# Attention followed by two feed-forward layers on one core: early input and weight sums around the second layer's tiles, and results leaving in other pieces

## The chip, the cores and the metric

One core of a Trainium2 chip runs the whole program. The metric is the device time of one execution in microseconds (us), the median over several runs. The engines are the matmul engine (PE, TensorE; its weight loads are listed as PEld), DVE (VectorE), ACT (ScalarE) and POOL (GpSimd); SP issues nearly all transfers, in the order of its own queue. Each engine takes its instructions in a fixed order, and an instruction that waits holds everything behind it on that engine.

## The reference

```python
attn = g * mem_out + (1 - g) * local       # 4 batches, 8 heads, 576 positions, 64 wide
x = attn.transpose(0, 2, 1, 3).reshape(2304, 512)
h = x @ w_in;   x = where(h > 0, h, exp(min(h, 0)) - 1) @ w_out     # layer 1, 512 -> 2048 -> 512
h = x @ w_in2;  out = maximum(0.01 * h, h) @ w_out2                 # layer 2, 512 -> 2048 -> 512
```

The local attention is causal, with a softmax; `mem_out` reads a memory matrix per head. Inputs and output are float32 (the weights come in as 64-bit floats and are unpacked on the chip). Only layer 2, and what is prepared for it in layer 1, is touched by the change.

## The kernel before

Every float32 operand of a matmul is split into a high part (rounded to fp32r) and a low part (the rest), and a product is made in three passes: high by high, low by high, high by low. ACT (or DVE) makes the high part as a copy, POOL (or DVE) the low part as a subtraction.

**Tiles.** After the attention, both layers run over five wide tiles of tokens, called T0 to T4 here (`gi` 0 to 4 in the code): four of 512 tokens and a last one of 256. Layer 1 goes over all five first and stores its results, x1, in DRAM (`x1_scr`, `x1s` in the trace). Then layer 2 goes over all five. The 2048 hidden columns are 16 blocks of 128, `f` = 0 to 15.

**Layer 2, plain tiles (T0, T1, T4).** For each f: 12 matmuls of 512 columns (L624) make the hidden block in a PSUM bank (tags `tp` and `pm`, two banks each); `leaky` makes its activation on ACT (L646) and DVE (L647), then the high part `gh` on DVE (L246) and the low part `gl` on POOL (L631). Two blocks later `emit_o3` feeds them into the output: four row blocks of 128 tokens, 12 matmuls of 512 columns per f (L987), into four banks (`sc` three times, `po` once) that add up over all 16 f.

**Layer 2, fast tiles (T2, T3).** Two hidden blocks are made together, as a 2 by 2 block product in seven products in place of eight (L1004; six matmuls of 256 columns each). That needs four sums of the two blocks' weights (`ws`) and four sums of the tile's inputs (the differences that `combine` makes), each again split in high and low. The products are added up on DVE (L1008) with copies on ACT; `rows` then makes the activation (L1012 DVE, L1015 ACT, L1016 POOL). In the first pair the products come in this order: a11 b11, a12 b21 (plain weights and inputs), then the ones with a weight sum: s4 b22, s1 t1, s2 t2, s3 t3, and at last a22 t4.

**What is prepared where.** `combine` (L936) runs in layer 1, one tile after T2 and T3: four DVE subtractions on the x1 tiles (L939), and four stores of the sums to DRAM (L940), per tile. `combine_w` (L948) makes the weight sums of the eight pairs of blocks during layer 2's T1, each tied behind the activation of a block f in `STEPS` = 0, 1, 2, 4, 5, 7, 8, 10. Each uses the one `wm` buffer: two additions (L955) and four of half the size (L957) on DVE, a copy on ACT (L960) into one of two input buffers (`xw1`, `xv1`), two subtractions on POOL (L962), a store to DRAM (L965). `load_ws` (L970) brings the sums of a pair back into one of the two `wraw` buffers; the first two pairs are loaded right at f = 0 and 1 of T1, the others two pairs ahead of their use.

**From one tile to the next.** `load3` (L851) is emitted near the end of a tile. It loads x1 of the next tile into the buffers `y` and `x` (L861; one buffer each) and splits it into `xh`, `xl` (L848 ACT, L849 POOL and DVE), which lie in `xw1`, `xv1` for all tiles but T1, and there in `xw0`, `xv0`. For a fast tile it then loads the input sums into the same `y` and `x` (L871) and splits them into `xw0`, `xv0`, all low parts on POOL. At a tile's end eight copies (L1081, DVE, 128 by 256 each) take the output banks through two `st` buffers to DRAM (L1082).

**Who sets the order.** The program is emitted in the order of the code; the framework then orders each engine's instructions by a simulated timeline and by priority, so that a load can be issued earlier than its place in the code. `behind_elu` (L879) keeps what it emits behind the last activation's instructions on the same engine.

Of the kernel before, what the change touches and what calls it, by code (L numbers as in the profile page):

```python
# [8 lines left out]
F32 = mybir.dt.float32  # L9
F32R = mybir.dt.float32r  # L10
# [9 lines left out]
def _f(ap):  # L20
    return ap.bitcast(F32)
# [3 lines left out]
def kernel(  # L25
# [135 lines left out]
    FAST = (2, 3)  # L161
    xt_scr = {gi: dram.tile([P, 4, 2, TW // 2], F32, name=f"xt{gi}") for gi in FAST}
    ws_scr = [dram.tile([P, 2, 4, 2 * P], F32, name=f"ws{i}") for i in range(NPR)]
# [687 lines left out]
    def load3(gi):  # L851
        w = wide[gi][1]
        xh, xl = (mtile(tag, 1, F32R, (NKC, TW))[:, :, 0:w] for tag in (("xw0", "xv0") if gi == 1 else ("xw1", "xv1")))
        for o in range(0, w if gi == 0 else 0, TN):
            st = mtile("x", 1, F32, (NKC, TN))
            nc.sync.dma_start(st, x1_scr[gi][:, :, o:o + TN])
            for c in range(NKC):
                split_to(xh[:, c, o:o + TN], xl[:, c, o:o + TN], st[:, c], nc.gpsimd)
        for e in range(2 if gi else 0):
            st = mtile("yx"[e], 1, F32, (2, w))  # L860
            nc.sync.dma_start(st, x1_scr[gi][:, 2 * e:2 * e + 2])  # L861
            for c in range(2):
                split_to(xh[:, 2 * e + c], xl[:, 2 * e + c], st[:, c], nc.vector if e else nc.gpsimd)
        if gi not in FAST:
            return xh, xl, None
        sums = []
        for e, tag in enumerate(("xw0", "xv0")):
            t = mtile(tag, 1, F32R, (NKC, TW)).rearrange("p a n -> p (a n)")
            t = t.rearrange("p (k l c n) -> p k l c n", k=2, l=2, c=2)
            st = mtile("yx"[e], 1, F32, (2, 2, TW // 2))  # L870
            nc.sync.dma_start(st, xt_scr[gi][:, 2 * e:2 * e + 2])  # L871
            for k in range(2):
                split_to(t[:, k, 0], t[:, k, 1], st[:, k], nc.gpsimd)
                sums.append((t[:, k, 0], t[:, k, 1]))
        return xh, xl, sums

    later = []

# [8 lines left out]
    for gi, (t0, w) in enumerate(wide):  # L887
# [9 lines left out]

        ys, yts = [], []

        def fetch_y():  # L900
            ne = NKC * TN // w
            for e in range(NKC // ne):
# [7 lines left out]
                ys.extend(yt[:, i] for i in range(ne))  # L910
                yts.append(yt)

        for f in range(NFA, NF):
# [6 lines left out]
            gs[f] = elu(ph, w)  # L920
            if later and f == NFA + (gi < 4):
                behind_elu(later.pop())
            if f > NFA + 1:
# [11 lines left out]

        def combine(gi=gi, yts=yts):  # L936
            b = [y[:, :, o:o + TW // 2] for y in yts for o in (0, TW // 2)]
            for k, o, x, y in ((0, 0, 1, 0), (3, 1, 3, 1), (1, 3, 3, 0), (2, 2, 2, 3)):
                nc.vector.tensor_tensor(out=b[o], in0=b[x], in1=b[y], op=ALU.subtract)  # L939
                nc.sync.dma_start(xt_scr[gi][:, k], b[o])  # L940

        if gi in FAST:
            later.append(combine)

    for u in w2:
        u()

    def combine_w(pr):  # L948

        m = pools["wst"].tile([P, 2 * DM], I32, tag="wm", bufs=pools["nwm"], name="wm")  # L950
        t = _f(m).rearrange("p (k n) -> p k n", k=4)
        for j in range(2):
# [3 lines left out]
        for o, a, b, op in ((3, 2, 3, ALU.add), (2, 0, 2, ALU.subtract), (0, 3, 0, ALU.subtract), (1, 1, 0, ALU.subtract)):  # L956
            nc.vector.tensor_tensor(out=t[:, o], in0=t[:, a], in1=t[:, b], op=op)  # L957
        v = mtile(("xw1", "xv1")[pr % 2], 1, F32R, (NKC, TW)).rearrange("p a n -> p (a n)")
        v = v.rearrange("p (l k n) -> p l k n", l=2, k=4)
        nc.scalar.copy(v[:, 0], t)  # L960
# [6 lines left out]
    uses = [(gi, pr) for gi in FAST for pr in range(NPR)]  # L967
    ws = {}

    def load_ws(key):  # L970
        raw = pools["wst"].tile([P, 2, DM, 2], I32, tag="wraw", bufs=2, name="wraw")
        v = raw.rearrange("p a n t -> p (a n t)").bitcast(F32R).rearrange("p (l k n) -> p l k n", l=2, k=4)
        nc.sync.dma_start(_f(v), ws_scr[key[1]])
        ws[key] = [v[:, :, k].rearrange("p l (c n) -> p l c n", c=2) for k in range(4)]

    STEPS = (0, 1, 2, 4, 5, 7, 8, 10)
    cur = load3(0)
    for gi, (t0, w) in enumerate(wide):
# [17 lines left out]

        xh, xl, sums = cur
        h = TW // 2
# [20 lines left out]
        for pr in range(NPR):  # L1019
            if gi in FAST:  # L1020
# [20 lines left out]
                add(u, product(a22, t4), u)  # L1041
                rows(2 * pr + 1, c1)
                at_use = uses.index((gi, pr)) + 2
                if at_use < len(uses):
                    load_ws(uses[at_use])
            else:
                for f in (2 * pr, 2 * pr + 1):
                    ph = h_bank()[:, 0:w]
                    h_mm(ph, wi_tiles[1, f], xh, xl)
                    gs[f] = leaky(ph, w)  # L1050
                    if gi == 1 and f in STEPS:
                        n = STEPS.index(f)
                        behind_elu(lambda: combine_w(n))
                        if n < 2:
                            load_ws(uses[n])
                    if f > 2 * pr and pr == NPR - 1:
                        break
                    if f > 1:
                        emit_o3(f - 2)
            if pr == NPR - 1 and gi + 1 < len(wide):  # L1060
                cur = load3(gi + 1)
            if pr == NPR - 1 or (pr and gi in FAST):
# [11 lines left out]
        for f in (NF - 2, NF - 1):  # L1074
            emit_o3(f)
        for tb in range(w // P):
            r0 = t0 + tb * P
            for hf in range(2):
                cs = slice(hf * DM // 2, (hf + 1) * DM // 2)
                o = mtile("st", 2, F32, (DM // 2,))  # L1080
                nc.vector.tensor_copy(o, pos[tb][:, cs])  # L1081
                nc.sync.dma_start(out[r0:r0 + P, cs], o)  # L1082

# [29 lines left out]
```

## Time and profile before

| | us |
|---|---|
| runs shown | 1077.43, 1077.97 (median), 1079.25 |
| the profiled execution's own time | 1078.21 |
| its span, first to last instruction | 1076.40 |
| busy time of the matmul engine in it | 1039.3 |

The profile shows one execution. "Busy" is the time in which an engine had an instruction under way; a wait is the idle time in front of an instruction, put down to what ended last before it. The granted clock of the matmul engine stands at 1.00 for 2.4 GHz and at 0.50 for 1.2 GHz; a stretch with a value between has parts at both. Layer 2 takes T1 from about 757 us on, T2 from about 845 us, T3 from about 940 us.

### The profile page before, as it was taken

The page shows a single profiled execution, that of the slowest core. Times are in us where ns is not written, and L with a number is a line of the kernel's source. Part 1 is how long each engine was busy: PE and PEld are TensorE (multiplying, and loading weights), DVE is VectorE, ACT ScalarE, POOL GpSimd, SP SyncE. Part 2 cuts the span into 40 slices and gives each one's busy share as a digit, 9 for nine tenths or more (in the row PEclk, how much of TensorE's full clock was granted, in tenths as well). Part 3 has the DMA queues.
Part 4 walks back from the last instruction along what each step waited for, and adds up shares of the span by engine and source line. Part 5 has one row for each costly group of instructions (what it writes and reads, how often), then busy time and mean ns, then how long its engine had stood idle before and what let it go on. Part 6 is the DMA issues. An engine that isn't in the chain of part 4 may idle for free. (4 is left out here: it accounts for less than half of the span.)

```text
span 1076.4 us, 18223 instructions
## 1 busy us (share of the span) xinstructions
PE 1039.3 (97%) x6192; PEld 921.6 (86%) x6192; DVE 679.3 (63%) x1524; ACT 513.7 (48%) x1223; POOL 552.7 (51%) x678
## 2 busy tenths in 40 slices
PE   6998999999999999999999999999999799999998
PEld 4776799989999999878888889788888688999897
DVE  6889987788888736566762426753565345454532
ACT  5999887787878635444442215332122221322211
POOL 7675775676767535455552217654345522432321
PEclk9999999999999999999999999999999999999999
DMA  7755543564455259456582305530252443452110
GB/s 183 196 144 117 161 140 101 128 167 141 122 128 146 90 136 342 146 194 201 186 274 79 118 4 174 176 117 0 79 195 118 133 141 107 139 159 87 40 40 20
DMA packets 154173, 144.47 MB, mean 134 GB/s; under 512 B 80608, under 2 KB 141024, under 8 KB 151008
## 3 DMA queue, kind: packets, MB, share of 16 engines
q1 hardware_dynamic: 153936, 143.04, 43.5%
q8 instruction: 49, 0.80, 0.3%
q14 instruction: 44, 0.36, 0.1%
q10 hardware_dynamic: 144, 0.26, 0.1%
HBM read 97.39 MB, written 42.34 MB: 130 GB/s over the span
## 5 line engine op out<-in xcount | busy, mean ns | idle before, releaser
L631 POOL TENSOR_TENSOR gl<-e,gh 128x512 fp32r<-128x512 f32 (+2 forms) x149 | 158.7, 1069 | 230.7 <-DVE gh L246 113.6
L987 PE MATMUL sc<-w,gh 128*128 128x512 f32 x448 | 136.7, 394 | 0.0
L454 POOL TENSOR_SCALAR pt<-pt,rs,omg 128x128 f32<-128x128 f32 (+4 forms) x160 | 103.3, 655 | 20.7 <-DVE rs L449 16.7
L624 PE MATMUL tp<-xw,w 128*128 128x512 f32 (+1 forms) x376 | 104.8, 360 | 1.5 <-DVE e L639 1.5
L624 PE MATMUL pm<-xw,w 128*128 128x512 f32 (+1 forms) x368 | 103.2, 362 | 1.2 <-ACT w L245 1.2
L439 ACT ACTIVATE pt<-pt,mx 128x128 f32<-128x128 f32 (+4 forms) x160 | 93.3, 584 | 23.0 <-DVE mx L434 21.5
L655 PE MATMUL sc<-gh,w 128*128 128x512 f32 (+2 forms) x438 | 103.2, 340 | 0.3 <-DVE gh L246 0.3
L1016 POOL TENSOR_TENSOR gl<-e,gh 128x512 fp32r<-128x512 f32 x32 | 41.6, 1300 | 114.9 <-ACT gh L1015 95.5
L987 PEld LDWEIGHTS sc<-w,gh 128*128 128x128 f32 x448 | 80.9, 190 | 13.7
L138 POOL TENSOR_TENSOR w<-wm,w 128x512 fp32r<-128x512 f32 x50 | 66.3, 1346 | 47.7 <-ACT w L245 39.5
L987 PE MATMUL sc<-w,gl 128*128 128x512 f32 x224 | 83.7, 393 | 5.1 <-POOL gl L631 5.1
L460 PE MATMUL tp<-ident,pt 128*128 128x128 f32 x480 | 83.1, 279 | 3.5 <-DVE al L253 1.5
L655 PEld LDWEIGHTS sc<-gh,w 128*128 128x128 f32 x438 | 74.6, 188 | 9.3 <-DVE gh L246 0.8
L624 PE MATMUL pm<-xh,w 128*128 128x288 f32 x368 | 80.3, 304 | 1.6 <-ACT xh L613 1.6
L624 PEld LDWEIGHTS tp<-xw,w 128*128 128x128 f32 x376 | 67.7, 189 | 13.0 <-DVE e L639 1.9
L624 PEld LDWEIGHTS pm<-xw,w 128*128 128x128 f32 x368 | 66.3, 189 | 12.7 <-ACT w L245 1.6
L434 DVE CUSTOM_DVE_ANT_0 pt<-sc,mask 128x128 f32<-128x128 f32 (+4 forms) x160 | 69.4, 445 | 7.5 <-PE sc L432 3.5
L460 PEld LDWEIGHTS tp<-ident,pt 128*128 128x128 f32 x480 | 59.6, 143 | 9.8 <-ACT ah L250 2.6
L624 PE MATMUL tp<-xv,w 128*128 128x512 f32 (+1 forms) x188 | 67.7, 360 | 0.0
L624 PE MATMUL pm<-xv,w 128*128 128x512 f32 (+1 forms) x184 | 66.5, 361 | 0.0
L655 PE MATMUL sc<-gl,w 128*128 128x512 f32 (+2 forms) x219 | 66.3, 340 | 0.2 <-POOL gl L631 0.2
L655 PE MATMUL pm<-gh,w 128*128 128x288 f32 x280 | 63.3, 306 | 0.0
(206 smaller groups left out, 2701.0 us busy)
## 6 DMA issues: line engine op xcount, KB each, us to landing
wraw<-in_moe_w_in_dram SPq DMA_DIRECT2D x32, 512.0 KB, 4.2
wraw<-in_moe_w_out_dram SPq DMA_DIRECT2D x32, 512.0 KB, 5.0
wraw<-ws SPq DMA_DIRECT2D x16, 1024.0 KB, 5.0
xh<-xh SPq DMA_DIRECT2D x8, 576.0 KB, 3.4
xl<-xl SPq DMA_DIRECT2D x8, 576.0 KB, 4.0
ys<-st SPq DMA_DIRECT2D x32, 144.0 KB, 2.8
vn<-in_v_dram SPq DMA_DIRECT2D x64, 64.0 KB, 2.6
out_dram<-st SPq DMA_DIRECT2D x32, 128.0 KB, 1.7
```

Of the source, the lines that this page charges most:

```text
L138: nc.gpsimd.tensor_tensor(out=w[:, 1, a], in0=t[:, a], in1=_f(w)[:, 0, a], op=ALU.subtract)
L434: nc.vector.tensor_tensor_reduce(out=pt[0:m, k0:k0 + n], in0=sc[0:m, 0:n], in1=mk, op0=ALU.add, op1=ALU.min, scale=-0.125, scalar=mx[0:m, ...
L439: nc.scalar.activation(out=pt[0:m, 0:nk], in_=pt[0:m, 0:nk], func=AF.Exp, scale=-1.0, bias=mx[0:m, last:last + 1], accum_out=self.pd["ss"] ...
L454: nc.gpsimd.tensor_scalar(out=pt, in0=pt, scalar1=rs[0:m, i:i + 1], scalar2=omg[0:m, h:h + 1], op0=ALU.mult, op1=ALU.mult,)
L460: nc.tensor.transpose(dst, self.p[c][:, k0:k0 + kn], ident)
L624: nc.tensor.matmul(ph, wi[:, wj, kc, :], xx[:, kc, :], start=n_mm == 0, stop=n_mm == 11)
L631: lo = nc.gpsimd.tensor_tensor(out=gl, in0=g, in1=_f(gh), op=ALU.subtract)
L655: nc.tensor.matmul(py, wo[:, wj, ec * P:(ec + 1) * P], gg, start=opens and f == first and n_mm == 0, stop=closes and f == last and n_mm == 2,)
L987: nc.tensor.matmul(pos[tb], gg[:, tb * P:(tb + 1) * P], wo[:, wj, :], start=f == 0 and n_mm == 0, stop=f == NF - 1 and n_mm == 2,)
L1016: nc.gpsimd.tensor_tensor(out=gl, in0=flat, in1=_f(gh), op=ALU.subtract)
```

## The change

In layer 1 `combine` goes. Everything else is in layer 2:

- During T1, behind f = 1, `sums_ahead` loads x1 of T3 into `y` and `x`, makes its four sums there in place and stores them to DRAM. Behind f = 3, `inputs_ahead` loads x1 of T2 into the same buffers, splits it into `xw1`, `xv1`, and makes T2's sums in place in `y` and `x`, where they stay.
- The weight sums are made in the two `wraw` buffers in place of `wm`, `xw1` and `xv1`, behind f = 0, 2, 4, 6, 8, 10, 11, 13; the first two loads of weight sums come behind f = 14.
- At the end of T1, `load_sums` splits T2's sums straight from `y` and `x`, with no load. At the end of T2 it loads T3's sums from DRAM.
- The results of T1 and T2 leave in other pieces: row blocks 0 and 1 as 128 by 512 copies through the `wm` buffer, row block 2 through the two `st` buffers as before, row block 3 (bank `po`) only behind the next tile's first pair of blocks. Loads of x1 in `fetch3` are queued behind the last result transfer emitted before them.

```diff
--- before.py
+++ after.py
@@ -159,7 +159,7 @@
     y_scr = [dram.tile([P, NKC, p[2]], F32, name=f"ys{i}") for i, p in enumerate(parts)]
     NPR = NF // 2
     FAST = (2, 3)
-    xt_scr = {gi: dram.tile([P, 4, 2, TW // 2], F32, name=f"xt{gi}") for gi in FAST}
+    xt_scr = dram.tile([P, 2, 2, TW], F32, name="xt")
     ws_scr = [dram.tile([P, 2, 4, 2 * P], F32, name=f"ws{i}") for i in range(NPR)]
     x1_scr = [dram.tile([P, NKC, min(TW, NT - t)], F32, name=f"x1s{t}") for t in range(0, NT, TW)]
 
@@ -856,25 +856,41 @@
             nc.sync.dma_start(st, x1_scr[gi][:, :, o:o + TN])
             for c in range(NKC):
                 split_to(xh[:, c, o:o + TN], xl[:, c, o:o + TN], st[:, c], nc.gpsimd)
-        for e in range(2 if gi else 0):
-            st = mtile("yx"[e], 1, F32, (2, w))
-            nc.sync.dma_start(st, x1_scr[gi][:, 2 * e:2 * e + 2])
+        rows = fetch3(gi) if gi else ()
+        for e, st in enumerate(rows):
             for c in range(2):
                 split_to(xh[:, 2 * e + c], xl[:, 2 * e + c], st[:, c], nc.vector if e else nc.gpsimd)
-        if gi not in FAST:
-            return xh, xl, None
-        sums = []
+        return xh, xl, rows
+
+    def fetch3(gi):
+        rows = [mtile(tag, 1, F32, (2, wide[gi][1])) for tag in "yx"]
+        with ExitStack() as order:
+            for ins in out_dmas[-1:]:
+                order.enter_context(tc.issue_after(ins))
+            for e, st in enumerate(rows):
+                nc.sync.dma_start(st, x1_scr[gi][:, 2 * e:2 * e + 2])
+        return rows
+
+    def add_rows(rows):
+        b = [y[:, :, o:o + TW // 2] for y in rows for o in (0, TW // 2)]
+        for o, i, j in ((0, 1, 0), (1, 3, 1), (3, 3, 0), (2, 2, 3)):
+            nc.vector.tensor_tensor(out=b[o], in0=b[i], in1=b[j], op=ALU.subtract)
+
+    def load_sums(rows):
+        if rows is None:
+            rows = [mtile(tag, 1, F32, (2, TW)) for tag in "yx"]
+            for e, st in enumerate(rows):
+                nc.sync.dma_start(st, xt_scr[:, e])
+        sums = {}
         for e, tag in enumerate(("xw0", "xv0")):
             t = mtile(tag, 1, F32R, (NKC, TW)).rearrange("p a n -> p (a n)")
             t = t.rearrange("p (k l c n) -> p k l c n", k=2, l=2, c=2)
-            st = mtile("yx"[e], 1, F32, (2, 2, TW // 2))
-            nc.sync.dma_start(st, xt_scr[gi][:, 2 * e:2 * e + 2])
             for k in range(2):
-                split_to(t[:, k, 0], t[:, k, 1], st[:, k], nc.gpsimd)
-                sums.append((t[:, k, 0], t[:, k, 1]))
-        return xh, xl, sums
-
-    later = []
+                split_to(t[:, k, 0], t[:, k, 1], rows[e][:, :, k * TW // 2:(k + 1) * TW // 2], nc.gpsimd)
+                sums[2 * e + k] = t[:, k, 0], t[:, k, 1]
+        return [sums[k] for k in (0, 3, 2, 1)]
+
+    out_dmas = []
 
     def behind_elu(unit):
         with ExitStack() as order:
@@ -895,7 +911,7 @@
                 o_mm(pys[ec], [f], 0, ec, gs, NFA, NF - 1)
             del gs[f]
 
-        ys, yts = [], []
+        ys = []
 
         def fetch_y():
             ne = NKC * TN // w
@@ -908,7 +924,6 @@
                             yt[:, :, lo - t0:hi - t0], y_scr[pi][:, ne * e:ne * e + ne, lo - tok:hi - tok]
                         )
                 ys.extend(yt[:, i] for i in range(ne))
-                yts.append(yt)
 
         for f in range(NFA, NF):
             if wun:
@@ -918,8 +933,6 @@
             ph = h_bank()[:, 0:w]
             h_mm(ph, wi_tiles[0, f], *cur)
             gs[f] = elu(ph, w)
-            if later and f == NFA + (gi < 4):
-                behind_elu(later.pop())
             if f > NFA + 1:
                 emit_out(f - 2)
             if gi >= 1 and f - NFA in (W2A, W2B) and len(w2) > NF - NFA:
@@ -933,30 +946,26 @@
             nc.vector.tensor_tensor(out=x1, in0=pys[ec], in1=x1, op=ALU.add)
             nc.sync.dma_start(x1_scr[gi][:, ec], x1)
 
-        def combine(gi=gi, yts=yts):
-            b = [y[:, :, o:o + TW // 2] for y in yts for o in (0, TW // 2)]
-            for k, o, x, y in ((0, 0, 1, 0), (3, 1, 3, 1), (1, 3, 3, 0), (2, 2, 2, 3)):
-                nc.vector.tensor_tensor(out=b[o], in0=b[x], in1=b[y], op=ALU.subtract)
-                nc.sync.dma_start(xt_scr[gi][:, k], b[o])
-
-        if gi in FAST:
-            later.append(combine)
-
     for u in w2:
         u()
 
+    ws = {}
+
+    def ws_tile():
+        raw = pools["wst"].tile([P, 2, DM, 2], I32, tag="wraw", bufs=2, name="wraw")
+        v = raw.rearrange("p a n t -> p (a n t)").bitcast(F32R).rearrange("p (l k n) -> p l k n", l=2, k=4)
+        return v, [v[:, :, k].rearrange("p l (c n) -> p l c n", c=2) for k in range(4)]
+
     def combine_w(pr):
 
-        m = pools["wst"].tile([P, 2 * DM], I32, tag="wm", bufs=pools["nwm"], name="wm")
-        t = _f(m).rearrange("p (k n) -> p k n", k=4)
+        v, _ = ws_tile()
+        t = _f(v)[:, 1]
         for j in range(2):
             w = _f(wi_tiles[1, 2 * pr + j])
             s = t[:, 2 * j:2 * j + 2].rearrange("p k (c n) -> p (k c) n", c=2)
             nc.vector.tensor_tensor(out=s, in0=w[:, 0], in1=w[:, 1], op=ALU.add)
         for o, a, b, op in ((3, 2, 3, ALU.add), (2, 0, 2, ALU.subtract), (0, 3, 0, ALU.subtract), (1, 1, 0, ALU.subtract)):
             nc.vector.tensor_tensor(out=t[:, o], in0=t[:, a], in1=t[:, b], op=op)
-        v = mtile(("xw1", "xv1")[pr % 2], 1, F32R, (NKC, TW)).rearrange("p a n -> p (a n)")
-        v = v.rearrange("p (l k n) -> p l k n", l=2, k=4)
         nc.scalar.copy(v[:, 0], t)
         for k in (0, 2):
             nc.gpsimd.tensor_tensor(
@@ -965,15 +974,29 @@
         nc.sync.dma_start(ws_scr[pr], _f(v))
 
     uses = [(gi, pr) for gi in FAST for pr in range(NPR)]
-    ws = {}
 
     def load_ws(key):
-        raw = pools["wst"].tile([P, 2, DM, 2], I32, tag="wraw", bufs=2, name="wraw")
-        v = raw.rearrange("p a n t -> p (a n t)").bitcast(F32R).rearrange("p (l k n) -> p l k n", l=2, k=4)
+        v, ws[key] = ws_tile()
         nc.sync.dma_start(_f(v), ws_scr[key[1]])
-        ws[key] = [v[:, :, k].rearrange("p l (c n) -> p l c n", c=2) for k in range(4)]
-
-    STEPS = (0, 1, 2, 4, 5, 7, 8, 10)
+
+    made = []
+
+    def sums_ahead(gi):
+        rows = fetch3(gi)
+        add_rows(rows)
+        for e, st in enumerate(rows):
+            nc.sync.dma_start(xt_scr[:, e], st)
+
+    def inputs_ahead(gi):
+        xh, xl, rows = load3(gi)
+        add_rows(rows)
+        made.append((xh, xl, rows))
+
+    AHEAD = {1: lambda: sums_ahead(FAST[1]), 3: lambda: inputs_ahead(FAST[0])}
+    for n, f in enumerate((0, 2, 4, 6, 8, 10, 11, 13)):
+        AHEAD[f] = lambda n=n: combine_w(n)
+    AHEAD[14] = lambda: [load_ws(u) for u in uses[:2]]
+    kept = []
     cur = load3(0)
     for gi, (t0, w) in enumerate(wide):
         pos = {}
@@ -994,7 +1017,8 @@
             for tb in range(w // P):
                 out_mm(f, tb, *g)
 
-        xh, xl, sums = cur
+        xh, xl = cur[0:2]
+        sums = cur[2] if gi in FAST else None
         h = TW // 2
 
         def product(wb, xb):
@@ -1040,6 +1064,8 @@
                 add(d, d, u)
                 add(u, product(a22, t4), u)
                 rows(2 * pr + 1, c1)
+                while kept:
+                    kept.pop(0)()
                 at_use = uses.index((gi, pr)) + 2
                 if at_use < len(uses):
                     load_ws(uses[at_use])
@@ -1048,17 +1074,16 @@
                     ph = h_bank()[:, 0:w]
                     h_mm(ph, wi_tiles[1, f], xh, xl)
                     gs[f] = leaky(ph, w)
-                    if gi == 1 and f in STEPS:
-                        n = STEPS.index(f)
-                        behind_elu(lambda: combine_w(n))
-                        if n < 2:
-                            load_ws(uses[n])
+                    if gi == 1 and f in AHEAD:
+                        behind_elu(AHEAD[f])
                     if f > 2 * pr and pr == NPR - 1:
                         break
                     if f > 1:
                         emit_o3(f - 2)
             if pr == NPR - 1 and gi + 1 < len(wide):
-                cur = load3(gi + 1)
+                cur = made.pop() if gi + 1 == FAST[0] else load3(gi + 1)
+                if gi + 1 in FAST:
+                    cur = cur[0], cur[1], load_sums(cur[2] if gi + 1 == FAST[0] else None)
             if pr == NPR - 1 or (pr and gi in FAST):
                 emit_o3(2 * pr - 1)
         if gi + 1 == len(wide):
@@ -1073,13 +1098,25 @@
             break
         for f in (NF - 2, NF - 1):
             emit_o3(f)
-        for tb in range(w // P):
+        if gi + 1 in FAST:
+            ends = _f(pools["wst"].tile([P, 2 * DM], I32, tag="wm", bufs=pools["nwm"], name="wm"))
+            for tb in range(2):
+                nc.vector.tensor_copy(ends[:, tb * DM:(tb + 1) * DM], pos[tb])
+                nc.sync.dma_start(out[t0 + tb * P:t0 + (tb + 1) * P, :], ends[:, tb * DM:(tb + 1) * DM])
+
+        def put(tb, pos=pos, t0=t0):
             r0 = t0 + tb * P
             for hf in range(2):
                 cs = slice(hf * DM // 2, (hf + 1) * DM // 2)
                 o = mtile("st", 2, F32, (DM // 2,))
                 nc.vector.tensor_copy(o, pos[tb][:, cs])
-                nc.sync.dma_start(out[r0:r0 + P, cs], o)
+                out_dmas.append(nc.sync.dma_start(out[r0:r0 + P, cs], o).ins)
+
+        for tb in range(2 if gi + 1 in FAST else 0, w // P):
+            if tb == 3 and gi + 1 in FAST:
+                kept.append(lambda put=put: put(3))
+            else:
+                put(tb)
 
 
 # ---- launch: one core; inputs and outputs as the reference has them ----
```

## Rows read from the trace of the kernel before

**Rows 1.** Page, part 1: busy time, share of the span, instructions.

```profile
PE 1039.3 (97%) x6192; PEld 921.6 (86%) x6192; DVE 679.3 (63%) x1524; ACT 513.7 (48%) x1223; POOL 552.7 (51%) x678
```

**Rows 2.** Waits of the matmul engine, 840 us to the end: total, times, longest.

```profile
PE sc L987 <- POOL gl L631: 3.8, 2, 3.2
PE pm L1004 <- DVE e L1008: 2.8, 1, 2.8
PE tp L1004 <- DVE e L1008: 0.7, 1, 0.7
```

**Rows 3.** Matmul engine, 836 to 885 us: start, length, line; [idle before].

```profile
842.17 0.62 PE L987 MATMUL sc<-w,gh 128*128 128x512 f32 x2
...
844.89 0.40 PE L1004 MATMUL pm<-xw,w 128*128 128x256 f32 x2
...
850.84 0.98 PE L987 MATMUL sc<-w,gl 128*128 128x512 f32 x3 [3.24 <-POOL gl L631]
...
855.16 0.88 PE L1004 MATMUL tp<-xv,wraw 128*128 128x256 f32 x6
855.88 0.88 PE L1004 MATMUL pm<-xv,w 128*128 128x256 f32 x6
...
860.27 0.50 PE L1004 MATMUL pm<-xw,w 128*128 128x256 f32 x2 [2.79 <-DVE e L1008]
...
861.99 0.50 PE L1004 MATMUL tp<-xw,wraw 128*128 128x256 f32 x2 [0.74 <-DVE e L1008]
```

**Rows 4.** POOL in order of time, 836 to 885 us.

```profile
848.30 1.26 POOL L849 TENSOR_TENSOR xv<-x,xv 128x512 fp32r<-128x512 f32 x1 [3.48 <-ACT xv L848]
849.52 1.27 POOL L631 TENSOR_TENSOR gl<-e,gh 128x512 fp32r<-128x512 f32 x1
```

**Rows 5.** SP's transfers in order of issue, 825 to 885 us.

```profile
837.11 0.32 SPq L965 DMA_DIRECT2D ws<-xv  x1
843.74 0.32 SPq L871 DMA_DIRECT2D x<-xt  x1
...
854.55 0.32 SPq L861 DMA_DIRECT2D y<-x1s  x1
854.97 4.94 SPq L1082 DMA_DIRECT2D out_dram<-st  x3
```

**Rows 6.** DVE in order of time, 825 to 885 us.

```profile
828.96 1.29 DVE L955 TENSOR_TENSOR wm<-w 128x512 f32<-128x512 f32 x2 [1.99 <-POOL xw L962]
...
837.80 0.43 DVE L246 CAST gh<-e 128x512 fp32r<-128x512 f32 x1
...
841.10 2.56 DVE L849 TENSOR_TENSOR xv<-x,xw 128x512 fp32r<-128x512 f32 x2 [1.14 <-DMA ws<-xv]
...
859.12 0.42 DVE L1081 COPY st<-sc 128x256 f32<-128x256 f32 x1 [5.80 <-DMA out_dram<-st]
```

**Rows 7.** Stretches: length, busy PE, PEld, DVE, ACT, POOL; granted clock, DMA share.

```profile
760.00:850.00 90.00, 87.04 (x386) 71.62 (x384) 55.56 (x90) 20.82 (x32) 45.72 (x35) 1.00 0.36 141
862.00:864.00 2.00, 2.00 (x9) 1.81 (x10) 1.86 (x4) 0.48 (x2) 1.35 (x1) 0.69 0.80 315
864.00:866.00 2.00, 2.00 (x9) 1.80 (x9) 0.29 (x1) 0.77 (x2) 0.93 (x1) 0.50 0.77 293
```

**Rows 8.** Matmul engine in order of time, 812 to 842 us.

```profile
827.45 0.39 PE L624 MATMUL tp<-xv,w 128*128 128x512 f32 x1
...
838.33 0.39 PE L624 MATMUL tp<-xv,w 128*128 128x512 f32 x1
```

**Rows 9.** Line 955: DVE additions, ns shortest/median/longest.

```profile
L955 DVE TENSOR_TENSOR wm<-w x16: 679/688/1775, 764.8 to 829.6; 128x512 f32<-128x512 f32 x16
```

**Rows 10.** Line 861: loads of a tile's rows, issue to landing.

```profile
DMA to landing us min/median/max: 2.9/3.6/5.3
```

**Rows 11.** Line 965: stores of weight sums, issue to landing.

```profile
DMA to landing us min/median/max: 3.8/3.8/4.9
```

**Rows 12.** Line 973: loads of weight sums, issue to landing.

```profile
DMA to landing us min/median/max: 4.6/5.0/8.5
```

## The prediction

> **What bounds the kernel now.** The page comes first: the matmul engine is busy for 97% of the span, with 6192 matmuls that the change neither adds to nor takes from [rows 1]. What can be had is the idle and slowed part of this engine, and only where it lies beside the work that the change touches. So the second view is the list of its waits from 840 us on, and there are three kinds: 3.8 us for POOL's low parts of the last hidden blocks of T1, and 2.8 and 0.7 us for DVE's additions [rows 2]. The engine's instructions in order of time put all of them at the passage from T1 to T2: a gap of 3.24 us, one of 2.79, one of 0.74 [rows 3].
>
> Then each gap is followed to its cause. The first waits for `gl` of the last block, which POOL did at 849.52, behind a split of T2's input sums that itself waited 3.48 us [rows 4]. That split needed the sums' load, which SP issued at 843.74, because the buffer was in use until then [rows 5]: DVE's splits of T2's inputs, which free it, began only at 841.10, after the last store of a weight sum out of the same buffers [rows 6]. The second gap waits for DVE, and DVE stood 5.80 us in front of a result copy at 859.12, since both `st` buffers were still on their way out [rows 6]. Why they were: SP issued the results from 854.97 on, behind a load of T3's inputs into `y` at 854.55 that had to wait until T2's sums in `y` were split [rows 5]. The third gap is DVE's backlog from the same stand. Last, the granted clock: it was 0.69 in 862 to 864 us and 0.50 in the next two [rows 7]. Against full speed that loses 2 x 0.31 + 2 x 0.50 = 1.62 us.
>
> The sum of what is lost at this one place is 3.24 + 2.79 + 0.74 + 1.62 = **8.39 us**, measured in an execution of 1078.21 us, 0.24 above the median of 1077.97; I take it off the median.
>
> **The change, part by part.** *T2's inputs and sums early.* The first gap's chain disappears: at the end of T1 no load and no split of T2's inputs is left, only the split of the four sums. These need the buffers that the last hidden matmuls of T1 read, free at about 838.7 [rows 8]. POOL then has four subtractions of 1.26 us and two `gl` of 1.27 [rows 4]: 7.6 us, to 846.3. The first use is late enough: in before, output block 14 took 842.17 to 844.89, 2.72 us [rows 3]; block 15 would end at 847.6, a product takes 0.72 us (855.16 to 855.88 [rows 3]), three come before the first with an input sum, so 849.8. So 3.24 us are gained.
>
> *Price of making them in T1.* DVE gets eight subtractions of 128 by 512. The nearest row is the addition of this size, 0.69 us in the middle [rows 9]: 5.5 us, against 55.6 busy of 90 in T1 [rows 7]. The chain through `y` and `x` is a load of 3.6 [rows 10], four subtractions, a store (no more than that of a weight sum, 3.8 [rows 11]) and a load of 3.6: 3.6 + 2.8 + 3.8 + 3.6 = 13.8 us, over some 60 us ahead of its use. Costed at nothing: the cover is the slack of the matmul engine in T1. That slack can be read: the last but two hidden block was ready at 827.8 [rows 8] and its `gh` only at 838.23 [rows 6], 10.4 us later, and the engine then waited just 0.6 [rows 2]. A longer hold would cost; that is rival 3. The same 0.6 us is not counted as a gain.
>
> The Trainium skill, "GPSIMD Engine Reference", section Specifications, says that GpSimd shares its SBUF interfaces with VectorE, and that instructions with two SBUF inputs contend; all added subtractions are of this kind and lie beside POOL's work. The trace agrees in part: the addition takes 0.68 to 1.78 us [rows 9]. If all eight took the longest, that would be 14.2 us, still inside DVE's room; what would come of it is lateness in T1, by that rule rival 2 rather than the forecast, 1073.3 rather than 1070.6.
>
> *Weight sums in `wraw`.* The same instructions, now without waiting for the one `wm`; against that, the last is tied to f = 13 and the first loads come at f = 14. In before the last sum took from 828.96 [rows 6] to its store at 837.11 [rows 5], 8.15 us. In the best case it starts two us behind f = 13's matmuls (an estimate from one DVE operation of 0.69, one of 0.43 and an ACT step of like size), 829.8, and is stored at 838.0; the first load is issued behind the store and lands 5.0 later [rows 12], at 843.3; the second waits for the store's 3.8 as well and lands at 846.8. They are needed at 847.6 + 1.44 = 849.0 and, a pair of seven products later, 854.1. Margins of 5.7 and 7.3 us; costed at nothing, with rival 2 for the loss of this cover.
>
> *Results in other pieces.* Row blocks 0 and 1 wait for no `st` buffer, block 2 has two free ones, block 3 comes a pair later. DVE so no longer stands in front of a result copy, and `y` and `x` are not asked for by SP before block 3 is out. This takes 2.79 and 0.74, and with the gaps the 1.62 of clock. The 128 by 512 copy itself isn't in the trace; four half copies of 0.42 [rows 6] are an upper bound for the two together, so DVE has no more to do than now. Nothing waits for the larger transfers in the tile.
>
> *Elsewhere.* `combine` and its stores leave layer 1, where the engine does not wait for them: nothing. The passage from T2 to T3 shows no gap [rows 2]: nothing.
>
> *What stays.* POOL's margin is 3.5 us of 849.8, and the order is planned anew; a small wait of 0 to 3 us at the passage is likely. I take 1.0, nearer the lower end, since every margin is positive by the median rows. **Sum: 1077.97 - 8.39 + 1.0 = 1070.6 us.**
>
> **Rivals.** *1, the forecast.* It goes from 1068.4 (no new wait, the 0.6 gone too, and some 0.6 for scatter, the runs' distance from the median downwards) to 1072.6 (3.0 left).
>
> *2, the weight sums come late.* If f = 13's `gh` is as late as in before (838.23), the last sum is stored at 846.4 and the first load lands at 846.7 + 5.0 = 851.7, 2.7 after it is needed; the second lands at 855.2, before 856.8. That gives 1073.3; with the longest load, 8.5 us [rows 12], 1076.8. For it: four of the eight sums are crowded behind f = 8 to 13. Against it: the lateness came of the single `wm` (DVE waited for POOL, 1.99 us at 828.96 [rows 6]), which is gone.
>
> *3, the change only moves the wait into T1.* T2's loads hang on T3's stores. If the high-part copies are placed on ACT where the chain begins, they hold ACT and the activations behind them for 13.8 us; beyond the 10.4 that cost 0.6, that is 4.0 us idle, and about 1.6 of clock as at 862: 1070.6 + 5.6 = 1076.2. Then the gain is hardly to be told from none.
>
> *4, slower: POOL serves T2's input sums before the last weight sum.* Both are ready at about the same time. Six operations of 1.27 in front put the store of rival 2 at 854.0, the load lands at 859.3, and the engine stands for 10.3 us at s4 b22, plus 1.6 of clock: 1070.6 + 11.9 = 1082.5. It decides as "slower" once that stand is over 7.9 us, a last store after 851.6. Against it: it takes the lateness of rival 2 as well, and the sums depend on matmuls that end after f = 13's.
>
> **How the numbers follow.** A measurement of this kernel can tell about 0.2%, 2.2 us, from no change; so faster is under 1075.8, slower over 1080.1. Forecast 0.60, rival 2 0.19, rival 3 0.10, rival 4 0.11. Rival 2 is faster in 0.16 and same in 0.03 of its cases, rival 3 faster in 0.03 and same in 0.07. Faster 0.79, same 0.10, slower 0.11. The range goes from the forecast's lower end to 1077.0, which takes in rival 2 with its longest load and the middle of rival 3, and leaves out rival 4, the upper part of rival 3 and a little below.
>
> **What would show it.** Right: no wait over 1 us of the matmul engine between T1 and T2; no load of input sums on SP there; DVE's result copies with no wait for transfers; granted clock 1.00 right through. Rival 2 or 4: a wait at the first products with `wraw`, released by a transfer, and the last store of a weight sum after 846 us. Rival 3: waits in T1 between 775 and 800 us, with ACT idle in front of a high-part copy. The prediction is wrong if the passage is clean and the time is not below 1075.8, or if layer 1 or T2's end show new waits.

## The result, and the profile after

The changed kernel takes 1068.25 us (median of six runs, 1067.66 to 1072.86), the kernel before 1077.71 (six runs, 1077.25 to 1079.25): ratio 0.9917, 95% interval 0.9900 to 0.9935, so 7 to 11 us faster. The forecast was 1070.6: direction and place were right, and the gain is 2 us larger. Against the range of 1068.4 to 1077.0 that is its lower edge: 0.9917 of the 1077.97 known then is 1069.0, just inside, while the median itself lies 0.15 us below it. The profiled execution is the longest of the six (1072.86); what it loses on the others lies ahead of layer 2. So times are compared below from one fixed point on: the 3700th of the 6192 matmuls, which lies in layer 1, behind the attention. It is found with the view of busy time by stretch, taken from 0 up to the time at which that many matmuls have begun: 611.21 us in this execution, 605 to 609 in the others. In the table, "last" is the start of the last matmul, and the times are of one profiled execution each; the changed kernel, profiled twice, gives 455.08 and 454.98. A time in this profile of the changed kernel is about 4.4 us later than the same place in that of the kernel before.

```
kernel            3700th   last    between   ratio of the runs, 95% interval
before            606.78  1070.76  463.98
changed           611.21  1066.29  455.08    0.9917  0.9900 to 0.9935
changed, again    607.64  1062.62  454.98    0.9917  0.9905 to 0.9928
e1_results        605.83  1063.77  457.94    0.9937  0.9925 to 0.9949
e2_old_results    608.02  1062.96  454.94    0.9909  0.9896 to 0.9922
e3_sums_by_dram   606.59  1061.96  455.37    0.9899  0.9886 to 0.9913
e4_weight_sums    608.92  1061.81  452.89    0.9894  0.9880 to 0.9908
e5_free_loads     606.97  1062.05  455.08    0.9910  0.9896 to 0.9923
e6_t3_in_layer1   606.83  1060.53  453.70    0.9893  0.9880 to 0.9907
e7_two_steps      607.35  1066.96  459.61    0.9954  0.9941 to 0.9967
e8_wm_scratch     606.97  1061.39  454.42    0.9892  0.9874 to 0.9910
e9_in_place       605.31  1060.86  455.55    0.9912  0.9895 to 0.9928
e10_sums_results  607.40  1059.86  452.46    0.9891  0.9876 to 0.9905
e11_no_subtr.     606.54  1058.34  451.80    0.9881  0.9863 to 0.9898
```

From there to the last matmul the change saves 8.9 us. The page's busy line, as in [rows 1], and the list of the matmul engine's waits from 590 us to the end, as in [rows 2], of the changed kernel:

```profile
PE 1039.5 (97%) x6192; PEld 922.8 (86%) x6192; DVE 689.9 (64%) x1520; ACT 513.8 (48%) x1223; POOL 558.0 (52%) x678
```

```profile
PE sc L1010 <- POOL gl L631: 2.9, 3, 1.3
```

The same list of the kernel before has 5.1 us for `gl` in layer 2, 1.3 more than [rows 2], which begins later; these are two waits in T0, at 694.85 and 697.40.

```profile
PE sc L987 <- POOL gl L631: 5.1, 4, 3.2
```

Of the waits before, those at the passage from T1 to T2 are gone, and so are the two of T0. New are three in T1. The engine's instructions in order of time, where [rows 3] shows the gaps:

```profile
798.62 0.50 PE L1010 MATMUL sc<-w,gl 128*128 128x512 f32 x1 [1.04 <-POOL gl L631]
...
821.26 0.50 PE L1010 MATMUL sc<-w,gl 128*128 128x512 f32 x1 [0.55 <-POOL gl L631]
...
839.16 0.50 PE L1010 MATMUL sc<-w,gl 128*128 128x512 f32 x1 [1.27 <-POOL gl L631]
...
844.07 0.39 PE L624 MATMUL tp<-xv,w 128*128 128x512 f32 x1
...
854.24 0.96 PE L1010 MATMUL sc<-w,gl 128*128 128x512 f32 x3
```

The line at 844.07 is the last hidden matmul of T1. The last line is the low-part pass of T1's last block, the one that waited 3.24 us in [rows 3]; it now has no wait. Busy time and clock by stretch at the passage, as in [rows 7]: busy throughout, and 1.00.

```profile
840.00:850.00 10.00, 10.00 (x47) 8.30 (x46) 5.49 (x8) 4.21 (x7) 7.08 (x6) 1.00 0.61 236
850.00:860.00 10.00, 10.00 (x73) 9.41 (x72) 5.58 (x13) 1.74 (x4) 4.82 (x5) 1.00 0.65 220
860.00:870.00 10.00, 10.00 (x64) 8.94 (x64) 6.31 (x12) 3.05 (x7) 3.29 (x3) 1.00 0.74 274
```

POOL in order of time, as in [rows 4], shows that the order which I had blamed is still there: the last `gl` of T1 (852.89) again stands behind T2's input sums, now behind all four splits (847.72 and 850.40, two each) and not behind one. It ends just as the engine needs it. Two things differ. The split in front of it no longer waits for what a load brings (3.48 us in [rows 4]), and this `gl` ends 9.7 us behind the last hidden matmul of T1 (844.46 to 854.19) in place of 12.1 (838.72 to 850.79, [rows 8] and [rows 4]). And the engine has more to do meanwhile: 22 matmuls of T2's first products stand in front of the low-part pass, in the kernel before six. Only the last four of the 22 take an input sum; the others take T2's plain inputs, with plain weights and with a weight sum.

```profile
843.73 2.77 POOL L971 TENSOR_TENSOR wraw<-wraw 128x512 fp32r<-128x512 f32 x2 [2.92 <-issue]
...
847.72 2.72 POOL L849 TENSOR_TENSOR xw<-y,xw 128x512 fp32r<-128x512 f32 x2
850.40 2.53 POOL L849 TENSOR_TENSOR xv<-x,xv 128x512 fp32r<-128x512 f32 x2
852.89 1.30 POOL L631 TENSOR_TENSOR gl<-e,gh 128x512 fp32r<-128x512 f32 x1
```

### The profile page after: what moved, and what is told of

It is laid out like the page before. It is cut to its first block, busy times and chain, and to the rows that moved or that the text cites. A ratio compares the mean times of both kernels' runs of the same rounds, so it can differ in the third digit from the quotient of the medians.

```text
span 1071.0 us, 18196 instructions
## 1 busy us (share of the span) xinstructions
PE 1039.5 (97%) x6192; PEld 922.8 (86%) x6192; DVE 689.9 (64%) x1520; ACT 513.8 (48%) x1223; POOL 558.0 (52%) x678
## 5 line engine op out<-in xcount | busy, mean ns | idle before, releaser
L631 POOL TENSOR_TENSOR gl<-e,gh 128x512 fp32r<-128x512 f32 (+2 forms) x149 | 163.1, 1099 | 221.5 <-DVE gh L246 109.5
```

What stands on the lines that cost most here:

```text
L631: lo = nc.gpsimd.tensor_tensor(out=gl, in0=g, in1=_f(gh), op=ALU.subtract)
```

## The experiments

The edits are shown shortened, by the lines that matter; `...` and the remarks behind `#` stand for what is left out. The names in the table are those of the kernels here, in short.

**The changed kernel again**, nothing edited.

> The changed kernel once more, nothing edited. The theory (the passage from T1 to T2 lost its three gaps and the half clock, 9.0 us with the 0.6 beside them, T0 lost 1.5 us of waits, T1 gained 2.9 us of new ones): 1068.2 us, ratio 0.991, and a profile with no wait of the matmul engine in T0 and about 2.9 us of waits for POOL in T1. Rival (the 3.4 us that the profiled execution lost ahead of layer 2 belong to the change): 1070 to 1073 us again.

1069.17 us (1067.86 to 1069.84), and the same three waits in T1, 2.7 us. The loss in the attention belongs to that one execution, not to the change.

**The results alone.** Edit, on the kernel before:

```diff
+        if gi + 1 in FAST:       # row blocks 0 and 1 through wm, block 3 behind the next pair
+            ends = ...
-            nc.sync.dma_start(st, x1_scr[gi][:, 2 * e:2 * e + 2])
+        rows = fetch3(gi)        # behind the last result transfer
```

> The kernel before, with only the results in other pieces and the loads of x1 queued behind them. The theory: it takes the second and third gap and the half clock, 2.79 + 0.74 + 1.62 = 5.2 us, and leaves the first of 3.24: 1072.6 us. Rival (the passage hangs on the weight sums leaving the input buffers): 1077.7, no difference. Rival (any one part clears the passage, since a single gap alone doesn't bring the clock down): under 1070.

Saved 6.0 us from the fixed point (5.2 expected), ratio 0.9937. The first gap stays and the other two are gone, as forecast for the parts; below, the matmul engine at the first gap and behind it, and the busy time and clock there.

```profile
849.37 0.97 PE L997 MATMUL sc<-w,gl 128*128 128x512 f32 x3 [3.17 <-POOL gl L631]
853.12 0.74 PE L1014 MATMUL pm<-xw,wraw 128*128 128x256 f32 x4 [0.17 <-POOL xw L849]
```

```profile
848.00:850.00 2.00, 0.63 (x3) 0.55 (x4) 0.10 (x1) 0.64 (x2) 2.00 (x3) 1.00 0.02 4
850.00:852.00 2.00, 2.00 (x17) 1.91 (x16) 2.00 (x5) 0.77 (x2) 2.00 (x3) 1.00 0.27 105
854.00:856.00 2.00, 2.00 (x19) 2.00 (x19) 2.00 (x6) 0.04 (x1) 0.00 (x0) 1.00 0.54 57
```

With the one gap of 3.17 us the clock stays at 1.00 here, so the 1.62 us of half clock in [rows 7] go with the second and third gap.

**The changed kernel with the old results.**

```diff
-        if gi + 1 in FAST: ...
+        for tb in range(w // P):   # eight copies through st, as before
```

> The changed kernel, with the results of T1 and T2 leaving as before (eight copies through the two small buffers, at the tile's end). The theory: DVE stands in front of result copies again, but no load into y is ahead of them on SP, so a part of the second gap comes back, 1 to 5 us: 1069.2 to 1073.4. Rival (the order on SP was enough, the pieces do nothing): 1068.2.

No difference: 1067.74 us, 454.94 from the fixed point. DVE waits for result transfers at this passage 1.8 us in all, against 8.1 in the kernel before, and the matmul engine has no wait there. Inside the changed kernel the new pieces are worth nothing that the runs can tell.

**The weight sums alone**, on the kernel before. The place of the sums, their scratch, their steps and their first loads change together.

```diff
-        m = pools["wst"].tile(... tag="wm" ...)        t = _f(m)...
-        v = mtile(("xw1", "xv1")[pr % 2], ...)
+        v, _ = ws_tile()                               t = _f(v)[:, 1]
-    STEPS = (0, 1, 2, 4, 5, 7, 8, 10)                  # with two loads at f = 0, 1
+    STEPS = (0, 2, 4, 6, 8, 10, 11, 13)                # with two loads at f = 14
```

> The kernel before, with only the weight sums made in the unpacking buffers, at the changed kernel's steps and with its late first loads. The theory: the first gap's chain begins earlier, as no store holds the input buffers of T2, but the load of the sums stays in it; the second gap stays whole: 1075 to 1077.7. Rival (the weight sums are what freed the passage): 1069 to 1070. Rival (the late first loads of weight sums cost on their own): over 1079.

The rival holds: 1066.76 us, ratio 0.9894, and 11.1 us saved from the fixed point on, where the whole change saves 8.9. The code that loads and splits T2's inputs was not touched, yet they are early all the same. There is no wait in T1 or at the passage (0.7 us lie in T0). ACT's instructions and SP's transfers of this kernel in order of time:

```profile
753.04 1.14 ACT L848 CAST xw<-y 128x512 fp32r<-128x512 f32 x2 [4.55 <-PE tp L624]
754.09 1.14 ACT L848 CAST xw<-x 128x512 fp32r<-128x512 f32 x2
```

```profile
757.31 0.33 SPq L871 DMA_DIRECT2D x<-xt  x1
757.74 0.79 SPq L871 DMA_DIRECT2D y<-xt  x1
```

T2's inputs are split at 753 us, at the end of T0, and the input sums are loaded at 757; in the kernel before, that load went out at 843.74 [rows 5]. With `xw1` and `xv1` free, the framework's own order brings both forward by 80 us and more.

**T2's input sums through DRAM**, in the changed kernel.

```diff
-        made.append((xh, xl, rows))                    # sums stay in y and x
+        nc.sync.dma_start(xt_scr[gi][:, e], st)        # and are loaded back, as T3's
```

> The changed kernel, with T2's input sums sent through DRAM and loaded back, as T3's are. The theory (what counts is that inputs and sums are ready long before the passage, not where they lie): the load back comes in T1 as soon as y and x are stored, so 1068.2 within 1 us. Rival (keeping them on chip is what closes the first gap): 3.2 us more, 1071.4.

1067.57 us, 455.37: no difference. Keeping them on chip is not what counts.

**The loads not queued behind the results**, in the changed kernel.

```diff
-            for ins in out_dmas[-1:]:
-                order.enter_context(tc.issue_after(ins))
```

> The changed kernel, with the loads of x1 no longer queued behind the last result transfer. The theory: at the passage SP again issues the loads of T3's inputs first and is held by the sums in y, but row blocks 0 and 1 don't use the small buffers, so DVE is held less: 0 to 3 us more, 1068.2 to 1071. Rival (the queue order is what removed the second gap): 5.2 more, 1073.4.

1068.61 us, 455.08: no difference either.

**T3's input sums in layer 1**, in the changed kernel.

```diff
-    AHEAD = {1: lambda: sums_ahead(FAST[1]), 3: lambda: inputs_ahead(FAST[0])}
+    AHEAD = {3: lambda: inputs_ahead(FAST[0])}
+        if gi == FAST[1]: later.append(combine)
```

> The changed kernel, with T3's input sums made in layer 1 again, behind the last tile's first block, and not in T1. The theory: T1 loses four subtractions, two loads and two stores, so its new waits of 2.9 us shrink by 1 to 2, and the waits of T0, 1.5 us, come back, since the work at the end of layer 1 is there again: 1066.5 to 1068.5. Rival (the new waits have nothing to do with T3's sums): 2.9 us of waits in T1 stay, 1068.2 to 1069.7.

1067.02 us, 453.70: the waits in T1 shrink from 2.9 to 1.0 us. T0's waits do not come back, so the work of T3's sums at the end of layer 1 was not their cause by itself (T2's sums are not made there in this kernel).

**Each weight sum in two steps**, in the changed kernel.

```diff
-        nc.scalar.copy(v[:, 0], t)                     # behind block f
+    def split_w(): ...                                 # copy, low part, store behind block f + 1
```

> The changed kernel, with each weight sum cut in two: the DVE additions behind block f, the copy on ACT, the low part on POOL and the store behind block f + 1. The theory (the waits in T1 come of ACT standing in front of a weight sum's copy, with the next activation behind it): they go, 1065.3 us. Rival (they come of DVE having too much to do): no change, 1068.2. Rival (the last sums now come too late for T2's first products): a wait at the first products with a weight sum, 1069 to 1073.

Worse than the changed kernel: 1073.42 us, 459.61, and none of the three expectations came out: the waits did not go, and all but 0.3 us of them lie at blocks of T1 and not at T2's products. ACT still stands in front of the copies. The list of ACT's waits in T1, first of the changed kernel, then of this one, where the copy has line 976 ("issue" is time in which ACT waited for nothing that the profile shows):

```profile
ACT wraw L969 <- issue: 28.1, 4, 7.5
ACT wraw L969 <- DVE wraw L968: 26.1, 4, 8.1
```

```profile
ACT wraw L976 <- DVE wraw L968: 34.6, 5, 9.1
ACT wraw L976 <- issue: 23.6, 3, 8.8
```

Together 54.2 us there and 58.2 here; what is put down to DVE grows from 26.1 to 34.6. So this cut did not free ACT, and it cannot say whether ACT's stand is what makes the waits in T1. The matmul engine waits for high and low parts at 844 us, and then its clock falls:

```profile
844.43 0.73 PE L1015 MATMUL sc<-w,gh 128*128 128x512 f32 x2 [1.47 <-DVE gh L246]
...
845.89 0.67 PE L1015 MATMUL sc<-w,gl 128*128 128x512 f32 x1 [0.72 <-POOL gl L631]
```

```profile
846.00:848.00 2.00, 2.00 (x5) 1.59 (x6) 0.12 (x1) 0.00 (x0) 2.00 (x2) 0.51 0.09 33
848.00:850.00 2.00, 2.00 (x8) 1.57 (x7) 0.00 (x0) 0.00 (x0) 2.00 (x3) 0.63 0.38 160
```

Half clock costs 2 x 0.49 + 2 x 0.37 = 1.72 us at that place. Why DVE is later in this order was not tried.

**The two things in the weight sums, one at a time.** First the weight sums' place: as in the weight sums kernel above, with its steps and late first loads, but with the scratch in `wm`.

```diff
+        m = pools["wst"].tile([P, 2 * DM], I32, tag="wm", bufs=pools["nwm"], name="wm")
-        t = _f(v)[:, 1]
+        t = _f(m).rearrange("p (k n) -> p k n", k=4)
```

> The kernel with only the weight sums moved to the unpacking buffers, but with its scratch in the one wm buffer as before, so that xw1 and xv1 are free and the single scratch stays. Theory now (the input buffers xw1, xv1 were held by the weight sums up to the passage; once free, T2's inputs are split and its sums loaded near 755 us by the order itself): passage clear, 1066.8 within 1.5. Rival (the single wm made the lateness): the gaps come back in part, 1070 or more.

1066.26 us, 454.42, no wait in T1 or at the passage: freeing the input buffers is enough (1.9 us of waits lie in T0). The later steps came along untested by themselves; they put the last sum behind f = 13 in place of 10, so they alone would hardly make anything earlier. Then the scratch alone: the kernel before, with the sums made in place in `xw1`, `xv1`.

```diff
-        t = _f(m).rearrange("p (k n) -> p k n", k=4)
+        t = _f(v)[:, 1]
```

> The kernel before, with the weight sums made in place in xw1 and xv1, so that wm is free and xw1, xv1 stay held up to the last store. Theory now: T2's inputs still wait for the last store, all three gaps stay, 1077.7 within 2. Rival (the single wm made the lateness): under 1073.

The rival holds here too: 1068.76 us, 455.55, with 1.8 us of waits in T1 and no gap at the passage. SP's transfers in order of time, to be read beside [rows 5]:

```profile
827.31 0.32 SPq L964 DMA_DIRECT2D ws<-xv  x1
833.63 0.32 SPq L871 DMA_DIRECT2D x<-xt  x1
834.75 0.32 SPq L871 DMA_DIRECT2D y<-xt  x1
842.99 0.32 SPq L861 DMA_DIRECT2D y<-x1s  x1
```

Without the one `wm` the last weight sum is stored at 827.31 and not at 837.11, and the input sums are loaded at 833.63 and not at 843.74. Of these 10 us the two profiles differ by 1.5 at the fixed point already, so the chain is between 8 and 9 us earlier. That clears the passage as well as taking the weight sums out of the chain.

**Weight sums and results together**, with the input sums in layer 1: the edits of the results alone and of the weight sums alone, both on the kernel before.

> The kernel before, with the weight sums in the unpacking buffers and the results in other pieces with the loads behind them, but with the input sums made in layer 1 as before. Theory now (the weight sums alone clear the passage, the results add nothing to it): 1066.8 within 1, no wait in T1. Rival (the two add up): 1065 or less.

1066.25 us, 452.46: the same as the weight sums alone, within what the runs can tell, and 0.3 us of waits in T1. The ratio to the kernel before is 0.9891, with an interval up to 0.9905; the changed kernel's two intervals begin at 0.9900 and 0.9905, so by the times alone the difference is just at what can be told. From the fixed point this kernel is 2.5 us shorter than the changed one, which is about the 2.9 us of new waits in T1. The early input sums are thus not needed here, and they cost about what they add in waits.

**The changed kernel without its subtractions.** Its edit:

```diff
-            nc.vector.tensor_tensor(out=b[o], in0=b[i], in1=b[j], op=ALU.subtract)
```

> The changed kernel without the eight subtractions that make the input sums in T1 (left out altogether, so the fast tiles' products take other inputs); loads, splits and stores stay. Theory now (the 2.9 us of new waits in T1 come of DVE's added work, behind which activations stand): at most 1 us of waits in T1, 1066. Rival (they come of the loads and splits, or of ACT's weight sum copies alone): 2.9 us of waits stay, 1068.2.

1065.08 us, 451.80, and no wait of the matmul engine after the attention. This kernel leaves out work that the result needs, so it is no version to use; it shows that the 2.9 us in T1 hang on the subtractions and not on the loads and splits. The step between is shown in part. In the changed kernel each of the three late `gl` stands on POOL behind the two low-part subtractions of a weight sum; POOL before the last of the three waits, whose `gh` was ready at 834.55:

```profile
834.67 2.76 POOL L971 TENSOR_TENSOR wraw<-wraw 128x512 fp32r<-128x512 f32 x2 [3.65 <-issue]
837.40 3.41 POOL L631 TENSOR_TENSOR gl<-e,gh 128x512 fp32r<-128x512 f32 x2
```

That order is also in the kernel without subtractions, where it costs nothing, so it is a matter of how late the blocks are. But the last subtraction ends at 806.26, 15 and 33 us ahead of the second and third wait; how the delay gets there, by a backlog or by another planned order, is not shown.

## Why the prediction was right in its number and wrong in its parts

**What bounds it: right.** 451.80 us is the stretch with no wait at all. The kernel before has 12.2 more, of which the list of waits and the half clock show 10.5; the changed kernel has 3.3, of which the list shows 2.9. The rest, 1.7 and 0.4 us, is explained in part only: a matmul behind a gap shows 0.50 us (798.62 above) where others show 0.39 [rows 8], so the seven gaps of the kernel before make about 0.8. The kernel with the loads not queued has 1.3 us of rest with two gaps; what that is stays open.

**The chain to the first gap: right, but cut at the wrong link.** The working followed it from `gl` back to the last store of a weight sum out of the input buffers [rows 4 to 6]. It then gave the 3.24 us to making T2's inputs and sums early and keeping them on chip. The runs show the link that counts: that last store. Taking the weight sums out of `xw1`, `xv1` clears the passage, and so does making them so that the last store comes 8 us earlier in the old place; where the input sums lie makes no difference. The prediction costed *Weight sums in `wraw`* at nothing, and that was the part that was enough. The step "T2's inputs and sums early" names an effect that the framework's order makes by itself once the buffers are free; whether making them early would do without moving the weight sums was not tried, and they need the same buffers.

**The second and third gap: a sufficient part taken for a necessary one.** The step gave 2.79 + 0.74 + 1.62 us to the results' pieces. Alone they do remove them. But they hang on the same late chain (the load into `y` that held SP waited for T2's sums), so moving the weight sums removes them as well, and in the changed kernel the old result copies cost nothing. The parts do not add up: alone they save 6.0 and 11.1 us, together 11.5.

**Costed at nothing, and not nothing: the price in T1.** "Costed at nothing: the cover is the slack of the matmul engine in T1" failed by 2.9 us in three waits. The slack of 10.4 us was read off a place with no added work; the subtractions stand in DVE's queue between weight sums and activations. Rival 3 had the place (T1) and the wrong holder: ACT stood 0.5 us in front of the copies of T2's inputs (793.71) and not 13.8, and of the waits at 798, 821 and 839 us only the first lies in its window of 775 to 800.

**Rivals 2 and 4: not met.** SP's transfers of weight sums at the passage:

```profile
841.37 0.32 SPq L980 DMA_DIRECT2D wraw<-ws  x1
846.53 0.32 SPq L974 DMA_DIRECT2D ws<-wraw  x1
850.42 0.32 SPq L980 DMA_DIRECT2D wraw<-ws  x1
```

The last store, at 846.53, is 842.1 in the times of the kernel before: later than the forecast's 838.0, earlier than rival 2's 846.4. The first load did not stand behind it, as the prediction had it, but went out 5.2 us ahead of it. Loads land 4.7 to 5.5 us after their issue, ahead of the first products with a weight sum at 853.00 and 859.10, and there is no wait at these. POOL served the last weight sum (843.73) before T2's input sums (847.72), the other way round than rival 4. The contention of the Trainium skill, "GPSIMD Engine Reference", section Specifications (GpSimd against VectorE's instructions with two SBUF inputs), is in the trace more clearly than I had it: the weight sums' additions no longer wait for POOL to end (idle 11.5 us before them, now 0.0), so more of them run beside its subtractions, and the 16 take 24.5 us in place of 15.7 (DVE by line and shape in T1, first of the kernel before, then of the changed one):

```profile
L955 DVE TENSOR_TENSOR wm<-w 128x512 f32<-128x512 f32 x16 | 15.7, 1022 | 11.5 <-POOL xw L962 7.9 <-POOL xv L962 3.5
```

```profile
L966 DVE TENSOR_TENSOR wraw<-w 128x512 f32<-128x512 f32 x16 | 24.5, 1570 | 0.0
```

They take as long in the kernel with weight sums and results together, which waits 0.3 us in T1, so the longer additions alone cost next to nothing here.

**What stays, and T0.** The 1.0 us for a new wait at the passage was 0, but POOL's margin of 3.5 us was not there: the four splits stood behind the last weight sum, and `gl` ended at 854.19 for a pass that began at 854.24. T0's 1.3 us fell away, which I had at nothing. T0's waits came out between 0 and 1.9 us in the kernels tried, with no part of the change that would decide it; that stays open.

**How much of the number was luck.** The 8.39 us were lost and gained as the sum had them. The rest came out near by terms that offset each other: 2.9 us of new waits in T1 against the 1.0 not needed, 1.3 of T0, 0.6 of the wait at 839.73 and 0.2 in layer 1, and 1.3 us that the list of waits does not show.

## What to carry to other kernels

Where several waits lie close together, follow each back as far as it goes before dividing the gain among the edits: here all led to one late store out of a borrowed buffer. An edit that is enough by itself need not be needed beside another; only making the parts one at a time, and taking them out one at a time, showed it. Scratch that borrows a buffer of the next stage sets when that stage can begin, and a framework that orders by itself will bring the stage forward once the buffer is free.

## What was not expected of the hardware

The granted clock fell to half after two waits of 1.47 and 0.72 us in the kernel with two steps, but stayed at 1.00 after a single gap of 3.17 us in the kernel with the results alone. So the length of the longest wait did not tell it in these runs. In both kernels where it fell, several waits followed one another; but in the kernel with the scratch in `wm`, two waits did so as well, and the clock stayed at 1.00:

```profile
695.63 0.96 PE L990 MATMUL sc<-w,gl 128*128 128x512 f32 x3 [1.26 <-POOL gl L631]
...
698.18 0.50 PE L990 MATMUL sc<-w,gl 128*128 128x512 f32 x1 [0.67 <-POOL gl L631]
```

```profile
694.00:698.00 4.00, 2.26 (x9) 1.24 (x7) 3.96 (x4) 0.60 (x1) 3.55 (x2) 1.00 0.38 131
698.00:702.00 4.00, 3.82 (x17) 3.19 (x18) 3.31 (x5) 1.55 (x2) 1.62 (x3) 1.00 0.34 101
```

What tells these cases apart was not found.
